# Weaving f32r transform matmuls between the 512-column matmuls of a second product, with a replanned order

## The chip, the cores and the metric

The kernel runs on one core of one Trainium2 chip. The metric is device time in microseconds, from one launch; the figure of a kernel is the median of its runs. One further execution was recorded by the profiler.

## The reference

The input is a sequence of 2048 rows of 640 channels in float32. Two kinds of layer alternate, twice each, with residual additions:

```
x = A_q
x = x + A(layernorm(x));  x = x + B(layernorm(x))
x = x + A(layernorm(x));  x = x + B(layernorm(x))

A(q): k_shift = causal convolution of k with 4 taps per channel
      kv = k_shift * v
      y  = causal convolution of kv with ssm_k (2048 taps per channel, by FFT) + kv * ssm_D
      return q * y
B(x): relu(x @ w1) @ w2        # w1 is 640 x 1728, w2 is 1728 x 640
```

The long convolution y depends on k, v and the kernels alone, not on x, so it is the same in both A layers.

## The kernel before

**Tiling.** The rows are cut into eight chunks of 256 (two halves of 128), the channels into five tiles of 128. For each chunk the kernel runs a "main" block per B layer: a first product (mm1, lines 1131 to 1157) into a PSUM tile h, relu on ScalarE into hh (the f16 value) with the remainder on VectorE into hl, and a second product (mm2, lines 1114 to 1129). Both products work with float16 pairs (value and remainder): three passes, high by high, high by low, low by high. The hidden width of 1728 is cut into seven pairs of 128 (indices j in the order JS, i = 0 or 1). In the second product the 128 rows of hh are the stationary operand and the 640 output columns stream past in two parts: 512 columns into a bank of their own (o) and 128 into a shared bank (oc). One mm2 step (one j, one i) covers one half (chunks 0 and 1, whose halves are separate blocks) or both halves of a chunk (chunks 2 to 7), so it has three or six 512-column matmuls and as many 128-column ones. Chunks 6 and 7 use another form of the second product (seven products in place of eight, lines 1059 to 1112), except for the pairs j in the tuple `plain` (line 1056), which are multiplied plainly; EARLY says how many of the first pairs are plain in the first layer of these two chunks. The seven products need sums of hidden halves (VectorE, lines 1232 to 1239) and sums of weights (wcombine, line 854).

**The convolution.** It works on "units": mostly pairs of a chunk and a channel tile, 21 units in all, counted in order by rank(u). For each, `transform` (line 438) forms kv with ScalarE and VectorE and transforms kernel and data with cosine and sine matrices on TensorE (tiles pg for the kernel, pr for the data); `products` (line 635) multiplies the transformed chunks on VectorE (pd, pacc), reading transformed chunks (Ax, Gx) back from memory by DMA, and transforms back on TensorE (tile pq). Each of the three transforms comes in two forms. The full one is a plain float32 matmul. The other, for units of two tiles with a rank of at least FA (pr), FU (pq) or FG (pg), splits data and matrix into two f32r parts (VectorE and ScalarE do the splitting, e.g. lines 585 and 723) and makes three f32r matmuls of 256 columns for each of four products: twelve in a chain, issued by `mm3` (lines 403 to 407).

**The order.** Nothing is issued while the work is being described. Every operation is recorded in a `Plan` with engine, assumed cost, tiles read and written, and a priority. `order` (line 209) plays the operations forward on assumed costs: whenever an engine is free it takes the ready operation with the smallest priority that fits into its tile rings. `latest` (line 172) goes backward through such an order and gives each operation the latest time at which it can run. `best` (line 144) alternates the two: a first order by fixed classes, then up to six more in which the latest times serve as priorities, and it keeps the order with the earliest assumed end. `issue` then emits all instructions in that order, each engine in its own queue; DMAs are issued by SP, some by GpSimd. An operation of TensorE is emitted whole: one mm2 step, one mm1 step, or one transform at a time.

```
    def mm3(o, c, i, xh, xl, first, last):
        ch, cl = c
        PE.matmul(o, ch[:, i, :], xh, start=first, stop=False)
        PE.matmul(o, ch[:, i, :], xl, start=False, stop=False)
        PE.matmul(o, cl[:, i, :], xh, start=False, stop=last)
```

Of the kernel before, what the change touches and what calls it, by code (L numbers as in the profile page):

```python
# [22 lines left out]
S = 2048  # L23
# [6 lines left out]
JS = (0, 1, 2, 3, 6, 4, 5)  # L30
# [8 lines left out]
NSPIN = 50  # L39
MMT = (0, 0.0558, 0.1092)  # L40
BM, BK = 1.7, 1.7
# [14 lines left out]
RENGS = ("PE", "ACT", "DVE", "POOL", "SP")  # L56
ENDS = []
# [19 lines left out]
WINO = ((6, 0), (7, 0), (6, 1), (7, 1))  # L77
EARLY = 1
ONPOOL = ()
# [25 lines left out]
class Op:  # L105
    __slots__ = ("eng", "cost", "fn", "prio", "seq", "deps", "outs", "new", "tiles", "left", "ready", "start", "nbytes", "late", "cls")


class Plan:
# [4 lines left out]

    def op(self, eng, cost, fn, reads=(), writes=(), prio=0, nbytes=0, late=0.0):
        o = Op()
        o.late = late
        o.eng, o.cost, o.fn, o.seq, o.nbytes = eng, cost, fn, len(self.ops), nbytes
# [25 lines left out]
    def best(self):  # L144

        tiles = list({id(t): t for o in self.ops for t in o.tiles}.values())
        rings = list({id(t.ring): t.ring for t in tiles if t.ring is not None}.values())
        kept = [(o, o.left, o.prio) for o in self.ops], [(t, t.left) for t in tiles], [(r, r.free, {k: list(v) for k, v in r.lines.items()}) for r in rings]
        found = None
        for n in range(PASSES + 1):  # L150
            if n:
                latest = self.latest(*last)
                for o, left, prio in kept[0]:
                    o.left, o.ready, o.start = left, 0.0, None
                    if prio[0] != CRIT and (o.eng in RENGS):
                        o.prio = (latest[o], o.seq)
                for t, left in kept[1]:
                    t.left = left
                for r, free, lines in kept[2]:
                    r.free, r.lines = free, {k: list(v) for k, v in lines.items()}  # L160
            try:
                last = self.order()
            except RuntimeError:
                break
            ENDS.append(last[1])
            if found is None or last[1] < found[1]:
                found = last + ([(o.start, o.ready) for o in last[0]],)
        for o, (a, b) in zip(found[0], found[2]):
            o.start, o.ready = a, b
        return found[:2]  # L170

    def latest(self, out, end):
# [5 lines left out]
        left, until = {o: len(o.outs) for o in out}, dict.fromkeys(out, end)  # L178
        before = {o: [(d, (0.0 if o.eng == "PE" else PEOUT) if d.eng == "PE" else 0.08 + RPE * (o.eng == "PE") * LATE(o)) for d in o.deps] for o in out}
        spare = {}  # L180
# [11 lines left out]
        open_, cur, latest = {}, {}, {}  # L192
# [16 lines left out]
    def order(self):  # L209
# [26 lines left out]
        now = 0.0  # L236
        while n < len(self.ops):
# [27 lines left out]
            for e in engs:  # L265
# [14 lines left out]
                if best is None:  # L280
                    continue
                cand[e].remove(best)
                for t in best.new:
                    t.ring.free -= 1
                    t.ring.lines[t.stream].pop(0)
                best.start = now
                free[e] = now + best.cost
                end = free[e] + (PEOUT if e == "PE" else 0.08)
                while best.nbytes and stalls and now >= stalls[0][0]:
                    dma = max(dma, now + DLAT) + stalls.pop(0)[1]  # L290
                if best.nbytes:
                    dma = max(dma, now + DLAT) + best.nbytes / (DBW0 if now < FIRST else DBW)
                    end = dma + (1.1 if e == "SP" else ALAT)
                best.ready = end
                if best.prio[0] == CRIT and e in soon:
                    soon[e].remove(best)
                if e == "PE":
                    for d in best.outs:
                        if d.eng == e:
                            d.left -= 1  # L300
                            if not d.left:
                                cand[e].append(d)
                heapq.heappush(finish, (end, best.seq, best))
                heapq.heappush(events, end)
                heapq.heappush(events, free[e])
                out.append(best)
                n += 1
        return out, now

    def issue(self):  # L310
        out, end = self.best()
        for o in out:
            for t in o.new:
                t.t = t.ring.pool.tile(t.shape, t.dtype, tag=t.ring.tag, name=t.name, bufs=t.ring.bufs)
            o.fn()
        return end


@with_exitstack
def tile_h3_mlp(ctx: ExitStack, tc: tile.TileContext, q, kT, vT, shk, hF, hR, dD, w1, w2, cM, cG, out):  # L320
# [20 lines left out]

    def pe(cost, fn, reads, writes, prio, late=0.0):
        plan.op("PE", cost, fn, reads, writes, prio, late=late)

# [58 lines left out]
    def mm3(o, c, i, xh, xl, first, last):  # L403
        ch, cl = c
        PE.matmul(o, ch[:, i, :], xh, start=first, stop=False)
        PE.matmul(o, ch[:, i, :], xl, start=False, stop=False)
        PE.matmul(o, cl[:, i, :], xh, start=False, stop=last)

# [29 lines left out]
    def transform(u):  # L438
# [60 lines left out]
        for j in range(1, 4):  # L499
            if u[0] in STT:  # L500
                for i, m, t in groups:

                    def f(i=i, m=m, t=t, j=j):
                        DVE.scalar_tensor_tensor(acc[:, i : i + m], kview(i, m, j), shs[:, t, j : j + 1], acc[:, i : i + m], op0=ALU.mult, op1=ALU.add)
# [30 lines left out]
        else:  # L535
            if rank(u) >= FG and n == 2:
# [4 lines left out]

                def f():
                    for ri in range(2):
                        for eo in range(2):
                            mm3(e4(pg[eo])[:, :, ri, :], cGs, 2 * eo + ri, gh[ri][:, eo], gl[ri][:, eo], ri == 0, ri == 1)

                pe(12 * mm, f, [*gh, *gl, *cGs], pg, pr_)
            else:
# [39 lines left out]

        def f(ris):
            for ri in ris:  # L590
                for kk in range(2):
                    o = pr[ri][:, 0:w].rearrange("p (c k e) -> p c k e", c=n, k=2)[:, :, kk, :]
                    if full:
                        PE.matmul(o, cMt[:, 2 * kk + ri, :], sh[:, ri, :], start=kk == 0, stop=kk == 1)
                    else:
                        mm3(o, cMs, 2 * kk + ri, sh[:, ri, :], sl[:, ri, :], kk == 0, kk == 1)

        if full:
            for ri in range(2):
                pe(8 * mm4, lambda ri=ri: f([ri]), [sh, cMt], [pr[ri]], pr_)  # L600
        else:
            pe(12 * mm, lambda: f([0, 1]), [sh, sl, *cMs], pr, pr_)
        for ri in range(2):
# [31 lines left out]
    def products(u, at, gt, after):  # L635
        n, nm = len(u), "%d_%d" % u[0]
        pr_ = (CRIT, CONV, LATER)[min(u[0][0], 2)]
        w, h = 2 * n * P, n * P
        mm, mm4 = (0.116, 0.113) if n == 2 else (0.213, 0.063)
        full = n == 1 or rank(u) < FU  # L640
# [47 lines left out]
        us = []  # L688
# [35 lines left out]
        if not full:  # L724

            def g():
                for ri in range(2):
                    o = pq[:, ri * 256 : ri * 256 + h]
                    for kk in range(2):
                        mm3(o, cMs, ri + 4 * kk, us[ri][0][:, :, kk, :], us[ri][1][:, :, kk, :], kk == 0, kk == 1)  # L730

            pe(12 * mm, g, [*us[0], *us[1], *cMs], [pq], pr_)
        if direct:
# [292 lines left out]
    def main(n, a, layer, S, xTS):  # L1026
# [87 lines left out]
        def mm2(j, i, hh, hl, SS=S):  # L1114
            tail = j == NFP - 1 and i == 1

            def f():
                wh, wl = (WT[j, 1, i][:, k, :] for k in range(2))
                for s in SS:
                    c = slice(i * R + (s - S[0]) * P, i * R + (s - S[0]) * P + P)  # L1120
                    for h in range(2):
                        d, z = ds[h], o(s, h)
                        end = j == JS[-1] and i == 1 and (h == 0 or s == S[-1])
                        PE.matmul(z, hh[:, c], wh[:, d], start=(j == JS[0] and i == 0 and (h == 0 or s == S[0])), stop=False)  # L1124
                        PE.matmul(z, hh[:, c], wl[:, d], start=False, stop=end and tail)  # L1125
# [3 lines left out]
            pe(0.136 * (4 if tail else 6) * len(SS), f, [hh, hl, WT[j, 1, i]], [*(ob[s] for s in SS), oc], FILL)  # L1129

# [344 lines left out]
```

## Time and profile before

| | before |
|---|---|
| median of 3 runs | 851.26 us (851.04 to 852.41) |
| profiled execution, its own time | 851.7 us |
| its span, first to last instruction | 849.8 us |
| granted TensorE clock | 1.000 |
| busy TensorE matmul / weight load | 839.6 / 666.7 us |
| busy VectorE / ScalarE / GpSimd | 755.7 / 494.1 / 46.1 us |
| DMA | 177.47 MB, mean 209 GB/s |

In the rows of the profile PE is TensorE's matmuls, PEld its weight loads (which run beside matmuls), DVE VectorE, ACT ScalarE. L405 is line 405 of the kernel. A row of a group reads: line, engine, operation, output tile <- input tiles, shapes, count | busy time in us, mean ns of one | idle time before. A row in order of time begins with the start and the duration in us; successive matmuls overlap, so what one costs is read from start to start. A row of waits reads: who waited <- for whom: total us, times, longest.

### The profile page before, as it was taken

To read this page: it belongs to the slowest core of one execution; us is meant where nothing else is said; L and a number is where in the kernel's file an instruction comes from. 1 tells how busy PE (TensorE), PEld (TensorE's weight loads), DVE (VectorE), ACT (ScalarE), POOL (GpSimd) and SP (SyncE) were. 2 spreads that over 40 slices of the span, in tenths; PEclk is the share of its full clock that TensorE was granted. 3 is DMA by queue.
4 is the path that set the end of the run, shared out by engine and by line. 5 is a ranking of instruction groups with operands and counts; after the bars stand their busy time and mean duration, and the time that the engine had idled before them with its cause. 6 is when DMAs were issued, how large, how long until landed. Compare 5 with 4: busy or idle time off the path is not lost.

```text
span 849.8 us, 19769 instructions
## 1 busy us (share of the span) xinstructions
PE 839.6 (99%) x7792; PEld 666.7 (78%) x7792; DVE 755.7 (89%) x1422; ACT 494.1 (58%) x1149; POOL 46.1 (5%) x57
## 2 busy tenths in 40 slices
PE   8999999999999999999999999999999999999998
PEld 7977888888787777777777777777777788888886
DVE  6999999999999999999999999999898689756544
ACT  5598587447586665637447375564515387647331
POOL 1000000000001101011010100010100000000000
PEclk9999999999999999999999999999999999999999
DMA  9995879889989999998996979497887374120100
GB/s 307 374 331 183 263 226 269 227 272 264 304 263 261 298 257 277 228 264 212 238 250 209 236 206 235 147 222 222 245 278 239 68 225 94 33 32 2 32 32 32
DMA packets 134128, 177.47 MB, mean 209 GB/s; under 512 B 50578, under 2 KB 88082, under 8 KB 134035
## 3 DMA queue, kind: packets, MB, share of 16 engines
q1 hardware_dynamic: 125714, 165.72, 64.8%
q0 software_dynamic: 8320, 10.49, 7.9%
q8 instruction: 61, 1.00, 0.5%
q14 instruction: 33, 0.26, 0.1%
HBM read 121.44 MB, written 34.08 MB: 183 GB/s over the span
## 4 chain that ended last, share of the span: by engine, by line
PE 74%; DVE 13%; DMA 5%; ACT 4%; issue 2%; SPq 0%; POOL 0%; DVEq 0%; ACTq 0%; POOLq 0%
PE h L1153 10%; PE h L1152 10%; PE h L1155 10%; PE o L1075 9%; PE o L1124 6%; PE o L1125 6%; PE o L1127 6%; PE pg L531 2%; PE oc L1124 2%; PE oc L1125 2%; DMA xT<-xh 2%; DVE pd L681 2%; PE oc L1127 1%; DVE pacc L682 1%; DVE hh L1242 1%
## 5 line engine op out<-in xcount | busy, mean ns | idle before, releaser
L1153 PE MATMUL h<-xT,w 128*128 128x256 f16 (+1 forms) x1290 | 301.4, 252 | 0.6 <-DMA xT<-xh 0.6
L1152 PE MATMUL h<-xT,w 128*128 128x256 f16 (+1 forms) x1290 | 301.7, 252 | 0.0
L1155 PE MATMUL h<-xT,w 128*128 128x256 f16 (+1 forms) x1290 | 301.4, 252 | 0.0
L1153 PEld LDWEIGHTS <-w 128*128 128x128 f16 x1390 | 136.0, 98 | 11.5 <-DMA xT<-xh 0.5
L1152 PEld LDWEIGHTS <-w 128*128 128x128 f16 x1390 | 136.0, 98 | 10.7
L682 DVE TENSOR_TENSOR pacc<-pacc,pd 128x768 f32<-128x768 f32 x140 | 133.9, 956 | 0.6
L1155 PEld LDWEIGHTS <-w 128*128 128x128 f16 x1290 | 126.2, 98 | 9.2 <-issue 0.4
L1125 PE MATMUL o<-w,hh 128*128 128x512 f16 x336 | 127.5, 379 | 0.9 <-DVE w L836 0.9
L1124 PE MATMUL o<-w,hh 128*128 128x512 f16 x336 | 127.6, 380 | 0.0
L1124 PEld LDWEIGHTS <-hh 128*128 128x128 f16 x672 | 65.7, 98 | 41.9 <-issue 0.9
L1125 PEld LDWEIGHTS <-hh 128*128 128x128 f16 x672 | 65.8, 98 | 40.9
L1241 ACT ACTIVATE hh<-h 128x512 f16<-128x512 f32 (+1 forms) x98 | 47.4, 483 | 78.9 <-PE h L1155 78.8
L681 DVE TENSOR_TENSOR pd<-Ax,Gx 128x768 f32<-128x768 f32 x83 | 78.7, 955 | 0.2
L1127 PE MATMUL o<-w,hl 128*128 128x512 f16 x208 | 78.9, 379 | 0.0
L1124 PE MATMUL oc<-w,hh 128*128 128x128 f16 x336 | 73.7, 219 | 0.0
L1125 PE MATMUL oc<-w,hh 128*128 128x128 f16 x336 | 73.7, 219 | 0.0
L1127 PEld LDWEIGHTS <-hl 128*128 128x128 f16 x416 | 40.7, 98 | 24.6
L473 ACT ACTIVATE tp<-kt,shs 128x256 f32<-128x256 f32 (+1 forms) x78 | 43.5, 575 | 19.0 <-DVE acc L510 16.7
L1127 PE MATMUL oc<-w,hl 128*128 128x128 f16 x208 | 45.7, 220 | 0.0
L681 DVE TENSOR_TENSOR pd<-at,Gx 128x768 f32<-128x768 f32 x46 | 43.2, 956 | 0.0
L1127 PE MATMUL o<-w,hh 128*128 128x512 f16 x104 | 39.4, 379 | 0.0
L1242 DVE SCALAR_TENSOR_TENSOR hl<-h,hh 128x512 f16<-128x512 f32 x50 | 34.5, 690 | 4.9 <-ACT hh L1241 4.6
(235 smaller groups left out, 1758.9 us busy)
## 6 DMA issues: line engine op xcount, KB each, us to landing
Ax<-A SPq DMA_DIRECT2D x89, 384.0 KB, 4.5
Gx<-G SPq DMA_DIRECT2D x89, 384.0 KB, 4.2
G<-gt SPq DMA_DIRECT2D x30, 384.0 KB, 4.7
A<-at SPq DMA_DIRECT2D x30, 384.0 KB, 5.3
ws<-in_w SPq DMA_DIRECT2D x28, 320.0 KB, 6.5
y<-Y SPq DMA_DIRECT2D x22, 320.0 KB, 3.9
x<-in_q SPq DMA_DIRECT2D x16, 320.0 KB, 4.5
gs<-in_hF SPq DMA_DIRECT2D x20, 256.0 KB, 5.2
```

Of the source, the lines that this page charges most:

```text
L473: ACT.activation(o[:, i : i + m], kview(i, m, j), AF.Copy, scale=shs[:, t, j : j + 1])
L681: ew(f"mac{j % POOLMOD}", 768, lambda e, pd=pd, av=av, gv=gv: e.tensor_mul(pd.t, av(), gv()), [ax, gx], [pd], pr_)
L682: dve(768, lambda i=i, pd=pd: DVE.tensor_add(acc[:, i], acc[:, i], pd.t), [acc, pd], [acc], pr_)
L1075: PE.matmul(b[:, c : c + w], x, y[:, z : z + w], start=done[i] == 1, stop=end, skip_group_check=fin)
L1124: PE.matmul(z, hh[:, c], wh[:, d], start=(j == JS[0] and i == 0 and (h == 0 or s == S[0])), stop=False)
L1125: PE.matmul(z, hh[:, c], wl[:, d], start=False, stop=end and tail)
L1127: PE.matmul(z, hl[:, c], wh[:, d], start=False, stop=end)
L1152: PE.matmul(p[:, z], wh, xv(t, 0), start=b, stop=False)
L1153: PE.matmul(p[:, z], wh, xv(t, 1), start=False, stop=tail and e)
L1155: PE.matmul(p[:, z], wl, xv(t, 0), start=False, stop=e)
L1241: act(2 * R, lambda p=p, hh=hh: ACT.activation(hh.t, p.t, AF.Relu), [p], [hh], URGENT)
L1242: dve(2 * R, lambda p=p, hh=hh, hl=hl: DVE.scalar_tensor_tensor(hl.t, p.t, 0.0, hh.t, op0=ALU.max, op1=ALU.subtract), [p, hh], [hl], URGENT)
```

## The change

1. `mm3`, the three f32r transforms and `mm2` now return their matmuls as lists of (columns, function), and an operation of TensorE may carry such a list (`parts`, marked "f" for a transform and "m" for an mm2 step).
2. When `order` gives TensorE an operation with parts, it looks for ready ones of the other kind. To an mm2 step it adds one transform and then, if there is one, a second mm2 step; to a transform it adds one mm2 step. The group is emitted as one: `weave` puts the transform's matmuls, in equal shares, behind each of the 512-column matmuls. Its assumed cost is worked out from column counts (`weave_cost`).
3. An mm2 step issues its 128-column matmuls ahead of its 512-column ones (WIDE_LAST).
4. `best` makes one first order, takes its latest times, adds to each a random number with a spread of 0.2 us (seed 42), and makes one second order, which is issued. In `latest`, what feeds a TensorE operation is due earlier: by 2.0 us when SP loads it, by 0.4 us when VectorE or ScalarE makes it (ROOM).
5. FA goes from 6 to 4, FU from 5 to 11, EARLY from 1 to 2. Three assumed costs are altered.

```diff
-MMT = (0, 0.0558, 0.1092)
+MMT = (0, 0.056, 0.1092)
-PASSES, RPE, RBW, RLAT = 6, 0.0, 330e3, 1.9
+RPE, RBW, RLAT = 0.0, 330e3, 1.9
+ROOM = {"SP": 2.0, "DVE": 0.4, "ACT": 0.4}
+SEEDS = (42,)
+WEAVE = {"m": 1, "f": 1}
+WIDE_LAST = 1
-FA = 6
-FU = 5
+FA = 4
+FU = 11
-EARLY = 1
+EARLY = 2
...
+        key = self.latest(*self.order())
+        for seed in SEEDS:
+            self.move(key, seed)
+        return self.again(kept, key)
+
+    def move(self, key, seed):
+        for o, d in zip(self.ops, np.random.default_rng(seed).normal(0, 0.2, len(self.ops))):
+            key[o] += d
...
-... else 0.08 + RPE * (o.eng == "PE") * LATE(o)) for d in o.deps] for o in out}
+... else 0.08 + (o.eng == "PE") * (RPE * LATE(o) + ROOM.get(d.eng, 0.0))) for d in o.deps] for o in out}
...
+                take(best)
+                if e == "PE" and best.parts:
+                    other = "mf"[best.parts[0] == "m"]
+                    if WEAVE[other]:
+                        while len(group) < 1 + WEAVE[other]:
+                            more = [o for o in cand[e] if o.parts and o.parts[0] == other and fits(o)]
+                            if not more:
+                                break
+                            group.append(min(more, key=lambda o: o.prio))
+                            take(group[-1])
+                        if other == "f" and len(group) > 1:
+                            more = [o for o in cand[e] if o.parts and o.parts[0] == "m" and fits(o)]
+                            if more:
+                                group.append(min(more, key=lambda o: o.prio))
+                                take(group[-1])
+                cost = best.cost
+                if len(group) > 1:
+                    best.woven = tuple(group[1:])
+                    cost = weave_cost(group)
+                free[e] = now + cost
...
+def weave(tr, pr, width):
+    wide = sum(width(x) == 512 for x in pr)
+    out = []
+    for x in pr:
+        out.append(x)
+        if width(x) == 512:
+            k = -(-len(tr) // wide)
+            out += tr[:k]
+            tr, wide = tr[k:], wide - 1
+    return out + tr
+
+def woven(group):
+    tr, pr = ([x for o in group if o.parts[0] == k for x in o.parts[1]()] for k in "fm")
+    return weave(tr, pr, lambda x: x[0])
+
+def weave_cost(group):
+    tr, pr = ([x for o in group if o.parts[0] == k for x in o.parts[2]] for k in "fm")
+    ns = weave(tr, pr, lambda x: x)
+    load = lambda n: 0.12 if n == 256 else 0.056
+    return sum(max(n / 2400 + 0.0025, load(m)) for n, m in zip(ns, (*ns[1:], 0)))
...
-        mm, mm4 = (0.116, 0.113) if n == 2 else (0.213, 0.063)
+        mm, mm4 = (0.1225, 0.1125) if n == 2 else (0.213, 0.066)
...
-                    for h in range(2):
+                    for h in (1, 0) if WIDE_LAST else (0, 1):
...
-                        PE.matmul(z, hh[:, c], wh[:, d], start=..., stop=False)
-                        PE.matmul(z, hh[:, c], wl[:, d], start=False, stop=end and tail)
-                        if not tail:
-                            PE.matmul(z, hl[:, c], wh[:, d], start=False, stop=end)
+                        passes = [(hh[:, c], wh[:, d]), (hh[:, c], wl[:, d])] + [(hl[:, c], wh[:, d])] * (not tail)
+                        for k, (x, y) in enumerate(passes):
+                            last = k == len(passes) - 1
+                            out.append(((512, 128)[h], lambda z=z, x=x, y=y, b=first and not k, e=end and last: PE.matmul(z, x, y, start=b, stop=e)))
```

More of the change, by code (lines that the diff above doesn't have):

```diff
@@ L54 @@
 ALAT = 3.1
-PASSES, RPE, RBW, RLAT = 6, 0.0, 330e3, 1.9
-RENGS = ("PE", "ACT", "DVE", "POOL", "SP")
-ENDS = []
+RPE, RBW, RLAT = 0.0, 330e3, 1.9
[3 more added lines that the diff above has]
+WIDE_LAST = 1
 def LATE(o):
@@ L105 @@
 class Op:
-    __slots__ = ("eng", "cost", "fn", "prio", "seq", "deps", "outs", "new", "tiles", "left", "ready", "start", "nbytes", "late", "cls")
+    __slots__ = ("eng", "cost", "fn", "prio", "seq", "deps", "outs", "new", "tiles", "left", "ready", "start", "nbytes", "late", "cls", "parts", "woven")
 class Plan:
@@ L113, in __init__, with op @@
         self.ops = []
-    def op(self, eng, cost, fn, reads=(), writes=(), prio=0, nbytes=0, late=0.0):
+    def op(self, eng, cost, fn, reads=(), writes=(), prio=0, nbytes=0, late=0.0, parts=None):
         o = Op()
-        o.late = late
+        o.late, o.parts, o.woven = late, parts, ()
         o.eng, o.cost, o.fn, o.seq, o.nbytes = eng, cost, fn, len(self.ops), nbytes
@@ L148, in best, with again @@
         kept = [(o, o.left, o.prio) for o in self.ops], [(t, t.left) for t in tiles], [(r, r.free, {k: list(v) for k, v in r.lines.items()}) for r in rings]
[L149 to L170, printed above, removed]
+        key = self.latest(*self.order())
[5 more added lines that the diff above has]
+            key[o] += d
+    def again(self, kept, key):
+        for o, left, prio in kept[0]:
+            o.left, o.ready, o.start, o.woven = left, 0.0, None, ()
+            if prio[0] != CRIT:
+                o.prio = (key[o], o.seq)
+        for t, left in kept[1]:
+            t.left = left
+        for r, free, lines in kept[2]:
+            r.free, r.lines = free, {k: list(v) for k, v in lines.items()}
+        return self.order()
     def latest(self, out, end):
@@ L178, in latest @@
         left, until = {o: len(o.outs) for o in out}, dict.fromkeys(out, end)
-        before = {o: [(d, (0.0 if o.eng == "PE" else PEOUT) if d.eng == "PE" else 0.08 + RPE * (o.eng == "PE") * LATE(o)) for d in o.deps] for o in out}
+        before = {o: [(d, (0.0 if o.eng == "PE" else PEOUT) if d.eng == "PE" else 0.08 + (o.eng == "PE") * (RPE * LATE(o) + ROOM.get(d.eng, 0.0))) for d in o.deps] for o in out}
         spare = {}
@@ L281, in order @@
                     continue
[L282 to L304, printed above, removed]
+                group = [best]
@@ new lines, in take @@
+                def take(o):
+                    cand[e].remove(o)
+                    for t in o.new:
+                        t.ring.free -= 1
+                        t.ring.lines[t.stream].pop(0)
+                    o.start = now
+                    if e == "PE":
+                        for d in o.outs:
+                            if d.eng == e:
+                                d.left -= 1
+                                if not d.left:
+                                    cand[e].append(d)
@@ new lines, in order @@
+                cost = best.cost
[3 more added lines that the diff above has]
+                free[e] = now + cost
+                for o in group:
+                    end = free[e] + (PEOUT if e == "PE" else 0.08)
+                    while o.nbytes and stalls and now >= stalls[0][0]:
+                        dma = max(dma, now + DLAT) + stalls.pop(0)[1]
+                    if o.nbytes:
+                        dma = max(dma, now + DLAT) + o.nbytes / (DBW0 if now < FIRST else DBW)
+                        end = dma + (1.1 if e == "SP" else ALAT)
+                    o.ready = end
+                    if o.prio[0] == CRIT and e in soon:
+                        soon[e].remove(o)
+                    heapq.heappush(finish, (end, o.seq, o))
+                    heapq.heappush(events, end)
+                    out.append(o)
+                    n += 1
@@ L311, in issue @@
         out, end = self.best()
+        done = set()
         for o in out:
-            for t in o.new:
-                t.t = t.ring.pool.tile(t.shape, t.dtype, tag=t.ring.tag, name=t.name, bufs=t.ring.bufs)
-            o.fn()
-        return end
+            if o in done:
+                continue
+            for x in (o, *o.woven):
+                for t in x.new:
+                    t.t = t.ring.pool.tile(t.shape, t.dtype, tag=t.ring.tag, name=t.name, bufs=t.ring.bufs)
+            if o.woven:
+                for _, f in woven((o, *o.woven)):
+                    f()
+                done.update(o.woven)
+            else:
+                o.fn()
+        return end
+def weave(tr, pr, width):
[16 more added lines that the diff above has]
+    return sum(max(n / 2400 + 0.0025, load(m)) for n, m in zip(ns, (*ns[1:], 0)))
 @with_exitstack
@@ L339, in keep, with pe @@
         return t
-    def pe(cost, fn, reads, writes, prio, late=0.0):
-        plan.op("PE", cost, fn, reads, writes, prio, late=late)
+    def pe(cost, fn, reads, writes, prio, late=0.0, parts=None):
+        plan.op("PE", cost, fn or (lambda: [f() for _, f in parts[1]()]), reads, writes, prio, late=late, parts=parts)
     def act(n, fn, reads, writes, prio, extra=0.0):
@@ L404, in mm3 @@
         ch, cl = c
-        PE.matmul(o, ch[:, i, :], xh, start=first, stop=False)
-        PE.matmul(o, ch[:, i, :], xl, start=False, stop=False)
-        PE.matmul(o, cl[:, i, :], xh, start=False, stop=last)
+        return [
+            (256, lambda: PE.matmul(o(), ch[:, i, :], xh(), start=first, stop=False)),
+            (256, lambda: PE.matmul(o(), ch[:, i, :], xl(), start=False, stop=False)),
+            (256, lambda: PE.matmul(o(), cl[:, i, :], xh(), start=False, stop=last)),
+        ]
     def pieces(u, ap):
@@ L1117, in f @@
             def f():
+                out = []
                 wh, wl = (WT[j, 1, i][:, k, :] for k in range(2))
```

42 lines of the change are left out of this document (23 added, 19 removed).

## The prediction

> **What bounds the kernel now.** I read the page first, then the busy time by stretches, then the waits of TensorE, then the order of time around the operations that the change touches.
>
> ```profile
> span 849.8 us, 19769 instructions
> PE 839.6 (99%) x7792; PEld 666.7 (78%) x7792; DVE 755.7 (89%) x1422; ACT 494.1 (58%) x1149; POOL 46.1 (5%) x57
> ```
>
> ```profile
> 50.00:62.00 12.00, 10.28 (x119) 7.31 (x117) 11.83 (x24) 11.86 (x24) 0.00 (x0) 1.00 1.01 306
> ...
> 350.00:450.00 100.00, 100.00 (x830) 77.10 (x829) 99.32 (x155) 55.47 (x125) 12.59 (x12) 1.00 0.92 239
> ...
> 800.00:849.80 49.80, 45.88 (x406) 37.86 (x404) 23.65 (x60) 11.32 (x21) 0.00 (x0) 1.00 0.07 27
> ```
>
> The columns of the stretches are length, then busy time of PE, PEld, DVE, ACT, POOL, then granted clock, DMA share and GB/s. TensorE is busy 839.6 of 849.8 us, and the whole 100 us in the middle. VectorE is there at 99.32 as well, but it does not hold TensorE up: nothing in that stretch is idle on PE. Of the 10.2 us that PE lacks, 1.72 lie at 50 to 62 us (where DVE and ACT are full with splitting the weights) and 3.92 in the last stretch, which is the closing VectorE work on the last chunk.
>
> ```profile
> PE o L1125 <- DVE w L836: 0.9, 2, 0.7
> PE hb L1254 <- ACT tb L1245: 0.8, 1, 0.8
> PE h L1153 <- DMA xT<-xh: 0.6, 2, 0.3
> PE pg L554 <- DVE ys L755: 0.4, 1, 0.4
> ```
>
> These are all the waits of TensorE after its start: 2.7 us. So a change of order can win at most about 3 us, and beyond that the time follows the sum of TensorE's work, one to one. The rest of the argument is that sum, taken from start to start of matmuls (the durations in the rows overlap).
>
> **The rows for the weaving.** A second product step without the change (L1124 to L1127), first 128 columns, then 512, then 128:
>
> ```profile
> 130.58 0.22 PE L1124 MATMUL oc<-w,hh 128*128 128x128 f16 x1
> ...
> 130.74 0.38 PE L1124 MATMUL o<-w,hh 128*128 128x512 f16 x1
> ...
> 131.39 0.22 PE L1124 MATMUL oc<-w,hh 128*128 128x128 f16 x1
> ```
>
> Three of 128 columns take 0.16 us (0.055 each), three of 512 take 0.65 (0.217 each). Now a transform's twelve f32r matmuls, after one f16 matmul of 128 columns, and their weight loads:
>
> ```profile
> 132.34 0.22 PE L1155 MATMUL h<-xT,w 128*128 128x128 f16 x1
> ...
> 132.57 0.28 PE L406 MATMUL pr<-sl,cMh 128*128 128x256 f32 x1
> ...
> 133.76 0.28 PE L407 MATMUL pr<-sh,cMl 128*128 128x256 f32 x1
> 133.88 0.23 PE L1152 MATMUL h<-xT,w 128*128 128x128 f16 x1
> 133.95 0.22 PE L1153 MATMUL h<-xT,w 128*128 128x128 f16 x1
> ```
>
> ```profile
> 132.34 0.19 PEld L405 LDWEIGHTS pr<-sh,cMh 128*128 128x128 f32 x1
> ...
> 133.64 0.19 PEld L407 LDWEIGHTS pr<-sh,cMl 128*128 128x128 f32 x1
> 133.88 0.10 PEld L1152 LDWEIGHTS <-w 128*128 128x128 f16 x1
> ...
> 676.71 0.19 PEld L407 LDWEIGHTS pq<-uh,cMl 128*128 128x128 f32 x1
> 676.95 0.10 PEld L1152 LDWEIGHTS <-w 128*128 128x128 f16 x1
> ```
>
> The same after one f16 matmul of 256 columns, where three of those take 0.33 us:
>
> ```profile
> 293.27 0.27 PE L1155 MATMUL h<-xT,w 128*128 128x256 f16 x1
> ...
> 293.60 0.27 PE L1155 MATMUL h<-xT,w 128*128 128x256 f16 x1
> ...
> 293.83 0.28 PE L406 MATMUL pr<-sl,cMh 128*128 128x256 f32 x1
> ...
> 295.14 0.39 PE L1124 MATMUL o<-w,hh 128*128 128x512 f16 x1
> ```
>
> Three things are to be seen. Inside the chain, f32r matmuls follow one another at (133.76 - 132.57) / 10 = 0.119 us, though 256 columns of f16 need only 0.11: the f32r weight load sets the pace. That load starts together with the matmul before it, f16 or f32r (132.34 and 132.34), and in both groups the second f32r matmul starts 0.23 after the last f16 one, whether that had 128 or 256 columns. So a 256-column f16 matmul hides an f32r load, and a 512-column one (0.217) would hide it wholly: this is the gain that the weaving aims at, 0.119 down to 0.109 for each. But going back to f16 costs: the f16 load does not start beside the last f32r matmul; it starts at 133.88, 0.12 after that matmul's start at 133.76, and the next f16 matmul comes 0.07 later where 0.055 is usual. The last group, at 676.7, shows the same (the f16 load is 0.24 behind the last f32r load, two steps of 0.12). The way back costs about 0.12 + 0.012 = 0.131 us for one f32r matmul, against 0.119 in the chain. Plain fp32 matmuls do not do this: behind the eight of L594 below, the f16 load starts at 91.92, 0.21 before its matmul at 92.13.
>
> A rule speaks against the change here. The Trainium skill, "TensorE: Matmul & The Clock Gate", "What overlaps and what doesn't", states that a weight load overlaps running matmuls only where the row group differs. The rows disagree for f32r loads, which start with the matmul before them, and agree only for the f16 load behind an f32r matmul; what the rule would make of the time is rival (e).
>
> So a chain of twelve costs now 133.88 - 132.34 - 0.055 + 0.012 = 1.50 us after 128 columns, and 295.14 - 293.60 - 0.11 + 0.01 = 1.44 after 256. Of the 40 chains, counted in order of time, 23 stand after 128 and 17 after 256: mean 1.474, or 0.123 for one matmul. Woven one by one behind twelve 512-column matmuls (two second-product steps and one transform), each f32r matmul is followed by an f16 one: 12 x 0.131 = 1.572, which is 0.10 more. In pairs (one step with six 512-column matmuls): 6 x (0.119 + 0.131) = 1.50, 0.03 more. In fours (the first two chunks, steps of three): 3 x (3 x 0.119 + 0.131) = 1.46, nothing.
>
> **The count.** The first matmuls of the f32r triples stand in three groups, four to a chain:
>
> ```profile
> L405 PE MATMUL pq<-uh,cMh 128*128 128x256 f32 x60 | 18.2, 303 | 0.0
> L405 PE MATMUL pr<-sh,cMh 128*128 128x256 f32 x60 | 18.2, 303 | 0.0
> ...
> L405 PE MATMUL pg<-gh,cGh 128*128 128x256 f32 x40 | 12.1, 303 | 0.0
> ```
>
> That is 15, 15 and 10 chains. FU = 11 takes units 6 to 10 out of pq (unit 5 has one tile and was full before), FA = 4 adds unit 4 to pr: 10 + 16 + 10 = 36 chains remain. About ten of them run in the first two chunks. Of the other 26 I take 16 as woven one by one, since the second-product steps stand ready in twos and fill half of TensorE's time there, and the rest in pairs or alone: 16 x 0.10 + 10 x 0.02 = +1.8 us. Bounds: nothing woven, 0; all 36 at 0.13 over a chain after 256 columns, +4.7; and if the way back cost nothing, 36 x (1.474 - 12 x 0.109) = -6.0.
>
> **FU and FA.** Full fp32 products:
>
> ```profile
> 90.35 1.95 PE L594 MATMUL pr<-sh,cM 128*128 128x256 f32 x8
> 92.13 0.38 PE L1124 MATMUL o<-w,hh 128*128 128x512 f16 x1
> ...
> 93.22 1.03 PE L716 MATMUL pq<-u,cM 128*128 128x256 f32 x4
> 94.09 0.38 PE L1124 MATMUL o<-w,hh 128*128 128x512 f16 x1
> ```
>
> ```profile
> 91.92 0.10 PEld L1124 LDWEIGHTS <-hh 128*128 128x128 f16 x1
> ```
>
> Eight take 92.13 - 90.35 = 1.78 us, four take 0.87. Five pq units go from 1.49 to 1.78: +1.45 us. One pr unit goes back from 1.78 to 1.50: -0.28. FU also takes ten VectorE subtractions away, and FA adds one:
>
> ```profile
> L723 DVE TENSOR_TENSOR ul<-u,uh 128x512 fp32r<-128x512 f32 x30 | 20.7, 690 | 0.1
> ```
>
> That is 9 x 0.69 = 6.2 us less VectorE work. I cost it at nothing, because TensorE does not wait for VectorE where those units run; it is a reserve only.
>
> **EARLY = 2.** In the blocks (6,0) and (7,0) one more pair of hidden columns is multiplied plainly:
>
> ```profile
> 685.15 0.44 PE L1075 MATMUL o<-w,hh 128*128 128x192 f16 x4
> ...
> 685.57 0.44 PE L1075 MATMUL o<-w,hh 128*128 128x192 f16 x4
> ...
> 686.81 0.43 PE L1075 MATMUL o<-w,hh 128*128 128x320 f16 x2
> ...
> 687.22 0.43 PE L1075 MATMUL o<-w,hh 128*128 128x320 f16 x2
> ```
>
> A split triple costs 0.42, an unsplit one 0.41. Plain: 4 + 4 triples, 4 x 0.42 + 4 x 0.41 = 3.32. By seven products: 0.42 + 6 x 0.41 = 2.88. Twice 0.44 is +0.88 us, all on TensorE, which has no gap in those blocks. The VectorE sums that it saves hide behind TensorE today.
>
> **128 columns first** moves matmuls inside a step: same count, same prices, 0. A chain that follows a step unwoven now stands behind 512 columns and costs 1.44 rather than 1.50, at most 0.6 us for ten of them, which I leave to the range.
>
> **Order and room.** The new order is one pass with scattered deadlines in place of the best of seven. On SP, loads that feed TensorE directly (xT, w) get due times 2.0 us earlier and pass the Ax, Gx loads and A, G stores in the queue; VectorE and ScalarE feeders get 0.4. Behind them wait VectorE's products, at 99.32 of 100 us. I take 0.45 of the 2.7 us of waits as won. Bounds: all 2.7 won, or as much as 8 lost (below). An f32r chain inside a step also puts its wait ahead of the step's later matmuls; the two chains above start with no wait, so I cost that at 0.
>
> **Sum:** 1.8 + 1.45 - 0.28 + 0.88 - 0.45 = +3.4 us. The profiled execution took 851.7 us with a span of 849.8, so it would be 855.1 with 853.2; on the median of 851.26 it is 854.7 us. About 0.2% (1.7 us) is what a measurement of this kernel can tell from no change.
>
> **Rivals.** (a) The way back is free: between two 512-column matmuls the f16 load slips in beside the f32r matmul, and it was the chain that held it back. For it: plain fp32 hides that load. Against it: both ends of chains shown, first and last. The time: 26 to 36 chains at -0.165 are -4.3 to -5.9, with the other terms -2.7 to -4.3, 848 us, faster. It decides below 0.118 us for one woven f32r matmul: at 312 of them, (0.123 - 0.118) x 312 pays the other +1.6. (b) The order loses: TensorE stalls for late VectorE results in woven groups, where 24 f16 matmuls stand behind a transform's operand, or for Ax, Gx pushed back. For it: VectorE at 99%, a single pass, operands used as soon as the plan has them. Against it: 6 us less VectorE work. At 0.2 us for each of 36 chains this is +7 to +8: 862 us. (c) The waits go wholly (2.7) and the weaving costs what I say: +1.2, 852.4. (d) The plan seldom finds a step and a transform ready together, so almost nothing is woven: +1.6, 852.9. (e) No weight load hides behind a running matmul: then an f32r one between 512-column ones would cost its load and itself, 0.119 + 0.131 = 0.25, and 312 of them +40 us, 891. The rows speak against it, since the f32r load starts with the f16 matmul before it. This is the rule of the Trainium skill named above.
>
> **How the numbers follow.** Forecast 0.55 (852.5 to 857), (a) 0.15, (b) 0.16, (c) 0.07, (d) 0.05, (e) 0.02. Faster by over 0.2% is (a) and the luckier part of (c): 0.18. Within 0.2%: the rest of (c), half of (d) and the low end of the forecast: 0.14. Slower: 0.68. The range runs from (a) at 848 to 860, which leaves out (e), the worse half of (b) and the best of (a).
>
> **What would show it.** Right: behind each woven f32r matmul the f16 load starts 0.12 after it and the next 512-column matmul 0.131 after it; L716 has 72 of 256 columns where it had 32; TensorE's gaps stay at about 10 us while its busy time rises by 3 to 4. Wrong: f16 loads that start with the f32r matmul, 0.109 for each, a TensorE busy time below 839; or new waits of PE on f32r operands or xT of several us.

## The result and the profile after

The changed kernel takes 853.48 us (median of 6 runs, 853.06 to 855.41), the kernel before 851.52 (6 runs). The ratio is 1.0028, 95% interval 1.0015 to 1.0041: 2.0 us slower, where +3.4 was forecast. The page of the changed kernel:

```profile
span 851.6 us, 19723 instructions
PE 842.0 (99%) x7788; PEld 672.8 (79%) x7788; DVE 750.6 (88%) x1408; ACT 488.8 (57%) x1137; POOL 45.8 (5%) x57
```

TensorE is busy 2.4 us longer, VectorE 5.1 us less. The busy time by stretches of the changed kernel:

```profile
50.00:62.00 12.00, 11.69 (x148) 8.96 (x146) 11.94 (x21) 11.93 (x24) 0.00 (x0) 1.00 1.07 317
...
350.00:450.00 100.00, 100.00 (x827) 78.01 (x826) 98.42 (x156) 53.52 (x115) 12.59 (x12) 1.00 0.90 235
...
800.00:851.60 51.60, 47.54 (x421) 39.16 (x419) 25.04 (x63) 11.99 (x22) 0.00 (x0) 1.00 0.07 27
```

The stretch from 50 to 62 us has 0.31 us of idle TensorE where it had 1.72, the middle is as full as it was, and the end has 4.06 idle where it had 3.92. The prediction's sign for being right, gaps of about 10 us and 3 to 4 us more of busy time, came out as 9.6 and 2.4. What TensorE waits for after its start:

```profile
PE h L1223 <- DVE hh L1313: 0.9, 1, 0.9
PE oc L1197 <- DVE x L1384: 0.3, 1, 0.3
PE oc L1197 <- DVE w L904: 0.3, 1, 0.3
PE oc L1197 <- DVE hh L1313: 0.2, 1, 0.2
```

They are 1.7 us, 1.9 with a wait for loads of weights, where it was 2.7, and no wait on xT is listed. Now a woven transform, one f32r matmul behind each 512-column one, first the matmuls, then the weight loads:

```profile
366.95 0.38 PE L1197 MATMUL o<-w,hh 128*128 128x512 f16 x1
366.98 0.47 PE L465 MATMUL pr<-sh,cMh 128*128 128x256 f32 x1
367.29 0.39 PE L1197 MATMUL o<-w,hh 128*128 128x512 f16 x1
367.32 0.47 PE L466 MATMUL pr<-sl,cMh 128*128 128x256 f32 x1
367.64 0.39 PE L1197 MATMUL o<-w,hl 128*128 128x512 f16 x1
...
367.99 0.28 PE L1197 MATMUL oc<-w,hh 128*128 128x128 f16 x2
```

```profile
366.95 0.19 PEld L465 LDWEIGHTS pr<-sh,cMh 128*128 128x128 f32 x1
367.28 0.10 PEld L1197 LDWEIGHTS <-hh 128*128 128x128 f16 x1
367.29 0.20 PEld L466 LDWEIGHTS pr<-sl,cMh 128*128 128x128 f32 x1
367.63 0.10 PEld L1197 LDWEIGHTS <-hl 128*128 128x128 f16 x1
```

(The recorded start of an f32r matmul behind a 512-column one is that of its load; the step is read from one 512-column matmul to the next.) From 366.95 to 367.99 are three pairs: 0.347 each, 0.216 of it for the 512 columns, 0.131 for the f32r matmul. Its own load starts with the f16 matmul and is hidden; the f16 load behind it starts only at 367.28, when the f32r matmul is through. A pair form, two f32r matmuls behind each 512-column one:

```profile
317.00 0.38 PE L1197 MATMUL o<-w,hh 128*128 128x512 f16 x1
317.03 0.47 PE L465 MATMUL pg<-gh,cGh 128*128 128x256 f32 x1
317.33 0.28 PE L466 MATMUL pg<-gl,cGh 128*128 128x256 f32 x1
317.45 0.39 PE L1197 MATMUL o<-w,hh 128*128 128x512 f16 x1
```

Here the second f32r load has only an f32r matmul to hide behind. Counted over all 36 chains in order of time (from the f16 matmul ahead of a chain to the second one behind it, less the f16 matmuls' own time): 8 chains woven one by one cost 1.594 us, 2 mixed ones 1.566, 15 in pairs 1.502, 4 in longer pieces 1.46 to 1.48, and 7 unwoven 1.442. The sum is 54.4 us, against 59.0 for 40 chains before.

```profile
L783 PE MATMUL pq<-u,cM 128*128 128x256 f32 x72 | 18.5, 384 | 0.0
```

The plain fp32 products of pq have gone from 32 to 72 instructions, as FU says. The whole difference of TensorE, from its first to its last start (843.6 to 845.3 us): chains -4.65, plain pq +8.9, plain pr -1.8, block (6,0) +0.43, and the waits, as what is left over, -1.2 (the listed ones, at the start and after it, fell by 1.1). That is +1.7; the span grew by 1.8.

### The profile page after: what moved, and what is told of

It reads as the page before. It is cut to its first block, busy times and chain, and to the rows that moved or that the text cites. A ratio compares the mean times of both kernels' runs of the same rounds, so it can differ in the third digit from the quotient of the medians.

```text
span 851.6 us, 19723 instructions
## 1 busy us (share of the span) xinstructions
PE 842.0 (99%) x7788; PEld 672.8 (79%) x7788; DVE 750.6 (88%) x1408; ACT 488.8 (57%) x1137; POOL 45.8 (5%) x57
## 4 chain that ended last, share of the span: by engine, by line
PE 84%; DVE 7%; DMA 5%; issue 1%; ACT 1%; SPq 1%; POOL 0%; DVEq 0%; ACTq 0%
PE o L1197 22%; PE h L1223 12%; PE h L1226 12%; PE h L1224 12%; PE o L1143 9%; PE oc L1197 6%; DMA Ax<-A 2%; DMA ws<-in_w 2%; PE pg L592 1%; DVE pd L748 1%; PE pq L783 1%; PE hb L1223 1%; PE hb L1224 1%; PE pt L640 1%; PE pr L656 1%
## 5 line engine op out<-in xcount | busy, mean ns | idle before, releaser
L1197 PE MATMUL o<-w,hh 128*128 128x512 f16 x776 | 235.1, 380 | 0.0
L1197 PEld LDWEIGHTS <-hh 128*128 128x128 f16 x1552 | 124.6, 98 | 68.0 <-DVE hh L1313 0.9
L1197 PE MATMUL oc<-w,hh 128*128 128x128 f16 x776 | 99.9, 220 | 1.0 <-DVE x L1384 0.3
L1313 DVE SCALAR_TENSOR_TENSOR hl<-h,hh 128x512 f16<-128x512 f32 x51 | 34.8, 682 | 10.2 <-ACT hh L1312 10.1
L1143 PE MATMUL o<-w,hh 128*128 128x320 f16 (+2 forms) x286 | 39.7, 257 | 0.0
L571 DVE TENSOR_TENSOR acc<-acc,tp 128x512 f32<-128x512 f32 (+1 forms) x54 | 36.0, 667 | 0.1
L552 POOL DMA_DIRECT2D gs<-hr x20 | 19.3, 963 | 312.2 <-DMA Ax<-A 184.7
L671 ACT ACTIVATE at<-pr 128x512 f32<-128x512 f32 (+1 forms) x42 | 23.4, 570 | 19.5 <-PE pr L467 16.9
```

Source lines behind the costliest of these rows:

```text
L571: ew(f"tap{j}", w, lambda e, tp=tp: e.tensor_add(acc.t, acc.t, tp.t), [acc, tp], [acc], pr_)
L671: act(w, lambda ri=ri: ACT.activation(at[:, :, ri, :], pr[ri][:, 0:w].rearrange("p (c b) -> p c b", c=n), AF.Copy), [pr[ri]], [at], pr_)
L1143: PE.matmul(b[:, c : c + w], x, y[:, z : z + w], start=done[i] == 1, stop=end, skip_group_check=fin)
L1197: out.append(((512, 128)[h], lambda z=z, x=x, y=y, b=first and not k, e=end and last: PE.matmul(z, x, y, start=b, stop=e)))
L1313: dve(2 * R, lambda p=p, hh=hh, hl=hl: DVE.scalar_tensor_tensor(hl.t, p.t, 0.0, hh.t, op0=ALU.max, op1=ALU.subtract), [p, hh], [hl], URGENT)
```

## The experiments

"Unwoven" means that the plan and its groups stay and only the order of emission inside a group changes.

**The weaving alone, e1_unwoven.**

```diff
-                for _, f in woven((o, *o.woven)):
-                    f()
+                group = (o, *o.woven)
+                steps, chains = ([x for x in group if x.parts[0] == k] for k in "mf")
+                for x in (*steps[:1], *chains, *steps[1:]):
+                    x.fn()
```

> The same plan and the same groups as the changed kernel, but a group is emitted one operation after the other: first second-product step, the transform's twelve matmuls in one chain, second step. Theory (the sum of TensorE's work sets the time, and each way back from f32r to f16 costs): the 36 chains cost 54.4 us in the changed kernel by its trace; unwoven, each stands behind a 512-column matmul and goes back to f16 once, 1.44 us, 51.9 in all. So 2.5 us less than the changed kernel, 851.0 us, TensorE busy about 839.5. Rival (the weaving pays, and the loss is made by the other parts): 0.119 in place of 0.109 for 432 matmuls, 4 us more, 857 us. Second rival (what counts is only the order of the plan, which stays): no change, 853.5.

Measured: 851.32 us (12 runs), ratio to the kernel before 1.0000 (0.999 to 1.001): 2.2 less than the changed kernel. The profiled execution is one of this kernel's longest (853.39) and is used for prices only. One of its chains:

```profile
504.14 0.38 PE L1199 MATMUL o<-w,hl 128*128 128x512 f16 x1
...
505.91 0.27 PE L1226 MATMUL h<-xT,w 128*128 128x256 f16 x1
```

Between the two stand the twelve f32r matmuls and one f16 matmul of 256 columns: 505.91 - 504.14 - 0.216 - 0.109 = 1.44 us for twelve, with one way back in place of up to twelve. All 36 chains sum to 51.9, as expected. The weaving itself loses 2.2 us; the first rival, by which it pays, is out, and so is the second.

**Three parts undone, e4_three_undone:** e1's edit, FU = 5, EARLY = 1.

> The changed kernel with the weaving, FU and EARLY undone (groups emitted one operation after the other, FU = 5, EARLY = 1); room, single pass, FA = 4 and 128 columns first stay. Theory (sum of TensorE's work): 2.5 less for the chains, 1.45 less for five pq products, 0.43 less for EARLY: 849.1 us, with TensorE's gaps as in the changed kernel. Rival (the 5 us of VectorE work that FU and EARLY take away is what shortened TensorE's waits by 1.2 us): the waits come back, 850.3 or more, with waits of PE on VectorE in the first 250 us.

Measured: 859.93 us (6 runs), ratio 1.0104 (1.0083 to 1.0124). The theory failed by 11 us. Its trace shows 6.2 us of TensorE's waits on xT, which neither theory had named, and a mean granted clock of 0.994 where the changed kernel's has 1.000. The rival was right that waits come back, but it looked for them before 250 us; the largest stand at 326 and 485 to 488 us.

**The planning alone, e5_order_alone:** e4's edits, FA = 6, WIDE_LAST = 0.

> Only the new planning is left of the change (room, one scattered pass, a transform placed beside a second-product step); weaving, FA, FU, EARLY and the column order are as before. Theory: TensorE has the work of the kernel before, chains mostly behind 128 columns (1.50 in place of a mean of 1.476, 0.6 more), waits 1.2 less: 850.9 us. Rival (the gain in waits came from VectorE's relief, not from the order): 852.1 or slower.

Measured: 858.49 us (6 runs), ratio 1.0076 (1.0061 to 1.009). With all work as before, the new planning is 7 us slower; 5.1 us are waits on xT. The rival's bound (852.1 or slower) holds; the theory's does not. The longest of these waits, 3.8 us, ends at 275.3, when a load of xT lands that SP had issued at 266.0, with xh written by 261.3: there VectorE was not late.

**Another seed, e6_seed43:** `SEEDS = (43,)`.

> The changed kernel with another seed for the scattered deadlines: same operations, another order. Theory: the same work of TensorE but for the number of ways back (a few tenths) and waits that differ by about 1 us: 852.5 to 854.5 us. Rival (the order, not the work, decides): more than 2 us away from 853.5, by waits of TensorE.

Measured: 853.86 us (6 runs), ratio 1.0029 (1.0017 to 1.004): the theory held, and the two seeds cannot be told apart here.

After these, FU and EARLY were taken back one at a time from the unwoven kernel, and each with both seeds.

**e7_unwoven_early1** (e1's edit, EARLY = 1) and **e10_early1_seed43** (the same with seed 43).

> The unwoven kernel with EARLY = 1: of the two that the run with three parts undone took back beside the weaving, only EARLY. Theory (the single pass needs the ten VectorE subtractions that FU = 11 spares, since VectorE is at 98% until 620 us; EARLY spares VectorE work only behind that): no xT waits in the first 620 us, three products of 320 columns less, 0.43: 850.9 us. Rival (it is EARLY that keeps the order free of waits): waits of PE on xT come, 855 us or more. Second rival (any new plan of this kind is a draw, with or without relief): 853 to 860, with waits in other places.

> The unwoven kernel with EARLY = 1, as before, and seed 43 in place of 42. Theory (each new plan of the single pass is a draw; EARLY itself is worth 0.43): the xT wait at 528 us does not come back in the same place; 851 to 856 us, most likely 852, with waits elsewhere. Rival (EARLY = 1 as such makes TensorE wait): 855 us or more, again with a wait on xT between 500 and 560 us.

Measured: 855.59 us (8 runs), ratio 1.0048 (1.0029 to 1.0067), and 855.12 (12 runs), ratio 1.0042 (1.0028 to 1.0056). The waits of TensorE in the one and in the other:

```profile
PE h L1226 <- DMA xT<-xh: 2.8, 1, 2.8
```

```profile
PE h L1226 <- DMA xT<-xh: 2.9, 1, 2.9
```

They stand at 529 and at 530 us, in the same place with both seeds: the rival held, not the draw. EARLY = 1 makes this planning 4 us slower, though the block it changes starts much later (in the kernel before, the first matmul of chunk 6's second product is at 685 us). VectorE is not the reason. In e7 it writes both halves of xh by 517.1 us, in e1 by 517.8. What differs is SP's queue. In e7 the last of the four loads of xT stands behind a load of hr (a kernel tile of the convolution), and that waits 2.8 us for the transfer gs<-hr out of the buffer that it is to fill:

```profile
515.54 1.55 DVE L1068 TENSOR_TENSOR xh<-xnB,xh 128x640 f16<-128x640 f32 x2
...
519.28 1.25 SPq L1080 DMA_TRANSPOSE xT<-xh  x1
...
525.05 0.38 SPq L522 DMA_DIRECT2D hr<-in_hR  x1
525.80 1.41 SPq L1080 DMA_TRANSPOSE xT<-xh  x1
```

In e10 it is the same (3.5 us, last load of xT at 527.63). With EARLY = 2, as here in e1, all four loads of xT go ahead of hr:

```profile
517.77 3.54 SPq L1080 DMA_TRANSPOSE xT<-xh  x2
...
526.82 0.38 SPq L522 DMA_DIRECT2D hr<-in_hR  x1
```

By these rows the wait comes from the order of loads that the planning makes, not from work that EARLY spares VectorE; a run with only that order changed was not made. Why EARLY shifts that order so far ahead of its own block stays open.

**e8_unwoven_fu5** (e1's edit, FU = 5) and **e11_fu5_seed43** (the same with seed 43).

> The unwoven kernel with FU = 5: five pq products of units 6 to 10 split again, 10 VectorE subtractions and 10 ScalarE copies more. Theory (VectorE's relief by FU is what keeps TensorE supplied): TensorE's work falls by 1.45, but waits of several us on xT between 130 and 500 us come: 856 to 859 us. Rival (EARLY is the cause, FU only costs): 849.9 us.

> The unwoven kernel with FU = 5 and seed 43. Theory (FU = 5 gives VectorE 6.9 us more to do before 320 us, where it is already full, and the single pass has no reserve): 857 to 863 us, waits on xT of several us whatever the seed. Rival (a draw as with EARLY): between 850 and 855 us with this seed.

Measured: 862.71 us (5 runs), ratio 1.0127 (1.011 to 1.0144), and 866.51 (5 runs), ratio 1.0172 (1.0149 to 1.0195). The theory named the waits rightly with both seeds, but both times lie about 3.5 us above its ranges. Waits of e8:

```profile
PE h L1225 <- DMA xT<-xh: 3.8, 2, 2.4
PE h L1226 <- DMA xT<-xh: 2.9, 2, 2.6
```

Here VectorE is late. Ahead of the largest wait, which ends at 488 us, it works without a gap from 469 us on and writes xh for this chunk 7 us later than in e1. VectorE in e8, then in e1:

```profile
474.62 1.55 DVE L1068 TENSOR_TENSOR xh<-xnB,xh 128x640 f16<-128x640 f32 x2
```

```profile
467.12 0.82 DVE L1068 TENSOR_TENSOR xh<-xnB,xh 128x640 f16<-128x640 f32 x1
468.46 0.81 DVE L1068 TENSOR_TENSOR xh<-xnB,xh 128x640 f16<-128x640 f32 x1
```

That is what FU = 5 gives VectorE more to do: by 467 us its subtractions ul <- u have taken 13.5 us in e8 and 6.8 in e1. The loads of xT follow late, the last one behind a load of Ax in SP's queue:

```profile
479.01 3.55 SPq L1080 DMA_TRANSPOSE xT<-xh  x1
482.67 0.52 SPq L738 DMA_DIRECT2D Ax<-A  x1
483.24 1.21 SPq L1080 DMA_TRANSPOSE xT<-xh  x1
```

The new planning has less room for this: of the 520 us between 100 and 620 us VectorE is idle for 10 in the kernel before, for 17 in the changed kernel, for 16 in e1 and for 18 in e8.

The waits are not the whole loss. Towards their end or right behind them the granted clock (the share of full speed that TensorE gets) falls, here in e8 (the 0.50):

```profile
490.00:492.00 2.00, 2.00 (x11) 1.45 (x10) 1.57 (x4) 0.89 (x3) 0.00 (x0) 0.50 1.11 361
```

It stays at 0.50 for 6.8 us, from 487.4 to 494.2, which by an estimate from the clock costs up to 3.4 us of TensorE's work. In the profiled executions e7 and e10 have 3.4 us at 0.50 behind their wait on xT; about the waits on xT of e4 it is 10.2 us, of e11 17.1. The five runs of e8 have mean clocks of 0.994 to 0.998, those of e11 0.990 to 0.994, those of e1 0.998 to 1.000. None of the theories had counted this.

**Relief without the new planning, e12_narrow_fu11:** the kernel before, 128 columns first (e9 below), FU = 11.

> The kernel before with the 128-column matmuls first and FU = 11, planned as before by the best of seven. Theory (the old planning finds an order without waits at full VectorE, so relief is worth nothing there): 1.45 more than with FU = 5, 852.2 us, VectorE busy about 749. Rival (relief shortens TensorE's waits in any planning): 850.8 or less.

Measured: 851.72 us (12 runs), ratio 0.9996 (0.9985 to 1.0007), 0.9 more than e9. The intervals of the two overlap, so what relief is worth under the best of seven (nothing by the theory, about 0.5 us by the medians) cannot be told from the noise. The rival has nothing for it: no run of e12 is as short as e9's median.

**Room without the single pass, e13_narrow_room:** the kernel before, 128 columns first, and only the ROOM term in `latest`.

> The kernel before with the 128-column matmuls first and only the room added to the deadlines (2.0 us for loads, 0.4 for VectorE and ScalarE), still the best of seven orders. Theory (room is no cause of its own; what made the other plans wait is the single pass): 849.5 to 852 us, waits of TensorE under 4 us after its start. Rival (room pulls xT and w ahead of Ax and Gx and VectorE starves): 855 us or more, with VectorE waiting for Ax or Gx by several us more than before.

Measured: 852.89 us (12 runs), ratio 1.0011 (0.9998 to 1.0025), 2.1 more than e9. This lies above the theory's range and below the rival's; VectorE waits 1.2 us for Gx, so it does not starve. Room does harm here, by small waits in several places: TensorE's after its start are 4.6 us where e9 has 2.6. Whether room helps under the single pass was not run, and neither was what the single pass and the scatter do by themselves.

**128 columns first alone, e9_before_narrow_first.**

```diff
-                    for h in range(2):
+                    for h in (1, 0):
                         d, z = ds[h], o(s, h)
```

> The kernel before, its plan untouched, with one edit: a second-product step issues its 128-column matmuls first, so that it ends on a 512-column one. Theory: the first f32r or fp32 load behind a step is then hidden. 15 f32r chains stand behind a step in the trace of before, 0.055 each, and eight fp32 products of pg, pq and pr, 0.055 each: 1.3 us less, 850.1 us. Rival (the start of the next operation was not on the path): no change, 851.4.

Measured: 850.78 us (11 runs), ratio 0.9986 (0.9975 to 0.9998). It is the one version faster than both kernels, by 0.6 us where 1.3 was expected. A chain of it, behind a step:

```profile
263.06 0.38 PE L1127 MATMUL o<-w,hh 128*128 128x512 f16 x1
...
264.78 0.22 PE L1153 MATMUL h<-xT,w 128*128 128x128 f16 x1
```

Less the 512-column matmul and one of 128 columns ahead of the last row, 264.78 - 263.06 - 0.216 - 0.056 = 1.45, where the same chain cost 1.50 behind 128 columns. All 40 sum to 58.2 in place of 59.0, the 0.8 expected of the chains. The other 0.5, expected of the fp32 products, does not show in the time, whose interval is about 2 us wide.

**The way back by itself, m1_way_back:** a small kernel of matmuls only; h is f16, b bf16, r f32r and x plain fp32. One stretch of it:

```
def s1():
    for _ in range(N):
        mm(pa, h, 512)
        mm(pb, r, 256)
```

> Not the reference's work: only TensorE matmuls on one tile, in nine stretches, start to start. First 48 f16 of 512 columns; then 24 pairs of one f16 of 512 and one of another kind: f32r 256, fp32 256, f32r 512, f32r 128; then bf16 512 with f32r 256; then fp32 256 with f32r 256; then 48 f32r 256 in a chain; last f16 of 512 on 64 stationary columns with f32r 256. Theory (the 128-column load of a 2-byte type does not run beside an f32r matmul, and that is all): f16 alone 0.216, pairs 0.216 + 0.133 = 0.349 with f32r 256, 0.216 + 0.24 with f32r 512, 0.216 + 0.08 with f32r 128, the same for bf16, 0.43 with fp32 (no way back), fp32 to f32r without a way back, chain 0.119, and on 64 columns no way back: 0.325. Rival (the change of type costs, whatever is loaded): the way back of 0.024 appears in the pairs with fp32 and on 64 columns too.

It ran once, with a granted clock of 1.00 in all stretches of pairs and in the chain. Two starts of the first matmul of a pair show the step, first f16 with f32r, then f16 with plain fp32:

```profile
19.63 0.39 PE L31 MATMUL pa<-h 128*128 128x512 f16 x1
19.66 0.47 PE L31 MATMUL pb<-r 128*128 128x256 f32 x1
19.97 0.39 PE L31 MATMUL pa<-h 128*128 128x512 f16 x1
...
30.10 0.38 PE L31 MATMUL pa<-h 128*128 128x512 f16 x1
30.31 0.59 PE L31 MATMUL pb<-x 128*128 128x256 f32 x2
30.75 0.38 PE L31 MATMUL pa<-h 128*128 128x512 f16 x1
```

Over 16 pairs of each: f16 with f32r 0.349, as expected; with f32r of 512 columns 0.460 and of 128 columns 0.291, so the f32r matmul costs 0.024, 0.029 and 0.020 (256, 512 and 128 columns) more than its columns; bf16 behaves as f16 (0.349). With plain fp32 the pair is 0.648, which is 0.216 and two instructions of 0.216 (I had counted one): no way back. fp32 with f32r is 0.547, where 2 x 0.216 + 0.109 would be 0.541: next to none. So the loss is that of a 2-byte load behind an f32r matmul; the rival, by which any change of type costs, is out by the pair with fp32. On 64 stationary columns both theories fail: the pair takes 0.647 (two starts: 86.46 and 87.11), twice their 0.325, and each load starts only with its own matmul (86.79 the f32r one). Why, stays open.

## Why the prediction was right, and where by luck

**TensorE's sum sets the time: right for the kernels compared.** TensorE is at 100.00 of 100 us in the middle of both, and taking 2.5 us of work away from it in e1 took 2.2 off the time.

**The way back: right.** Forecast 0.131 for a woven f32r matmul, measured 0.131 in the rows and 1.594 for twelve (1.572 forecast); pairs 1.502 (1.50), pieces of four 1.46 (1.46). **The count was off:** 8 chains one by one, not 16. The weaving term was therefore +1.25 against the chains of before (+1.8 forecast).

**FU and FA: right in TensorE's work** (72 instructions; 1.45 and -0.28 by the traces). **EARLY: half.** The step "in the blocks (6,0) and (7,0)" misread the condition `a < NC - 1` at line 1056, which leaves (7,0) out; measured +0.43, not +0.88.

**Waits: -1.2, forecast -0.45, and the reason was wrong.** The step that failed is "a reserve only": FU's relief of VectorE was costed at nothing because TensorE did not wait for VectorE before. That was true of the old order. Under the new planning, FU = 5 costs 11 us against e1 (e8), and 15 with the other seed (e11; e1 itself was run with seed 42 alone), in waits on xT and in the lower clock behind them, with xh 7 us late. EARLY = 1 costs 4 us (e7, e10) by another way, the order of loads on SP, which the prediction named as a risk for Ax and Gx and not for xT. So the two parts that looked like pure cost kept the new planning free of these waits. Rival (b), +7 to +8 by stalls on late VectorE work, is much like the outcome of the change without these two; its price of 862 is near e4's 859.9, though it placed the stalls in woven groups.

**The nearness was in part luck.** The waits did not come since FU and EARLY were in the same change, not for a reason that the prediction gave. Against the forecast the smaller weaving, half of EARLY and the better waits make up -1.7, and 0.3 the other way came from the end and the medians.

**128 columns first: "0", left to the range.** It is worth 0.6 us alone (e9), and e1's chains behind a step cost 1.44 by it.

## What to carry to other kernels

Before a slow weight load is woven behind wide matmuls, look in the trace at the step back as well: here each return from f32r to f16 cost more than the hidden load saved, and one long chain behind a wide matmul was the cheapest form. A wide matmul ahead of such a chain can be had by turning a loop round, without any weaving. When a change swaps the planner and relieves a second engine that is nearly full, cost the relief under the new plan: an engine at 98% that nobody waits for can be the bound in the next order. When a load comes late, look at the queue that issues it before blaming the engine that made its data, and count the granted clock behind a wait as well as the wait.

## What the runs showed of the hardware

A weight load of a 2-byte type (f16, bf16, 128 columns) started beside a running f16 or plain fp32 matmul, but not beside an f32r one: the f32r matmul of 256 columns then costs 0.131 to 0.133 us rather than 0.109. An f32r load does run beside f16 and f32r matmuls, and sets the pace at 0.119 to 0.120 in a chain. With 64 stationary columns of f16 in the pair, the time doubled to 0.647 us at a granted clock of 1.00, unexpected and unexplained. Towards the end of eight waits or pairs of waits on xT of 2.0 to 7.3 us (e4, e7, e8, e10, e11), or right behind them, the granted clock fell to 0.50 for 3.4 or 6.8 us; with two others (2.6 us in e8, 3.8 in e5) it stayed at 1.00.
